# Feature exponent of a linear-attention kernel: norm, maximum and sign in one fused VectorE operation per head, with a new plan

## The chip, the core and the metric

The kernel runs on one core of one Trainium2 chip. The metric is device time in microseconds of one execution of the whole program. A core has TensorE (PE, matrix products into PSUM), VectorE (DVE), ScalarE (ACT), GpSimd (POOL) and SyncE (SP, which here issues every DMA). Each engine works through its own instructions in order, and semaphores order the engines among each other.

## The reference, cut to what matters

An attention in linear form (random exponential features) is followed by two multilayer perceptrons. Everything is float32; q and k are scaled, features are taken, and the attention output of shape 2304 x 512 passes through both perceptrons.

```python
def phi(x):                                    # x: 4 batches, 8 heads, 576 tokens, 64
    proj = np.einsum('bhsd,md->bhsm', x, omega)          # 128 features
    sq = np.sum(x * x, axis=-1, keepdims=True) / 2.0
    h = proj - sq
    h = h - np.max(h, axis=-1, keepdims=True)
    return np.exp(h) / np.sqrt(m)
q_p, k_p = (phi(q_s), phi(k_s))
kv = np.einsum('bhsm,bhsd->bhmd', k_p, v)
z = np.sum(k_p, axis=2)
num = np.einsum('bhsm,bhmd->bhsd', q_p, kv)
den = np.einsum('bhsm,bhm->bhs', q_p, z)[..., None] + 1e-06
x = num / den
h = x @ w_in;  g = h * np.tanh(log(1 + exp(h)));  x = g @ w_out      # 512 -> 2048 -> 512
h = x @ w_in2; g = h * sigmoid(h);                out = g @ w_out2
```

## The kernel before, in words

The kernel does not run in loops over the chip's time. It registers some thousands of small tasks (one or a few instructions each) with a planner, and the planner then writes them out in an order of its own.

**The attention.** There are 36 k units and 36 q units, each of 128 tokens by four heads. A k unit (`k_unit`) loads its tile (`kin`, DMA, ring of 5 buffers), sums the squares of its 4 x 64 columns per head (`sums`: on VectorE four multiplications with a running sum, L459; or on GpSimd and a VectorE reduction, L441 and L442; or on ScalarE, L451), projects it on TensorE (L500) into a PSUM bank `kpj`, and passes the bank to `softmax_part`. There VectorE takes the maximum over 128 features for each of the four heads in one reduction (L466), and two small operations on 128x4 (L469, L471) make the bias from the sum of squares and the maximum. ScalarE then takes four exponentials of 128x128 out of the PSUM bank into the SBUF buffer `kf` (L476; 4 buffers for k, 3 for q, where the buffer is `qf`). TensorE accumulates the outer products of the features with v and their sum (L511); at the end of a group `k_finish` copies the state and spreads the sums z (L532, L536, L542). A q unit (`q_unit`) is the same up to its exponential; then come the product with z and its sum, the denominator (`den`: on VectorE four multiplications with a running sum, L608; or on GpSimd, L592, with a VectorE reduction, L604), the small constant added (L616), the reciprocal (L617), the normalisation (L626 on GpSimd or VectorE, L623 on ScalarE), four transposes on TensorE (L633), and after every second unit the product with the state (L657), which gives x as a high and a low part (L667, L671).

**The perceptrons.** All float32 products are made of three passes over high and low parts (`mm3`, L275 to L277). Weights arrive as 64-bit numbers and are converted by ScalarE and VectorE (L690, L693, L698, L701) and split (L709, L711). The first perceptron's first half of hidden units (phase 0) is worked while the attention still runs, one 256-token block after another; phases 1 to 4 follow on pairs of blocks with pre-added operands (L717, L735, L849) and end at the last store.

**What sets the order.** `Plan.add` gives each task an engine, a modelled cost and a key (a due time, shifted by the table `OFF` by name or by kind). `Plan.order` walks a model of the engines: among the tasks that can start within `EPS` of the earliest one it takes that with the lowest key, no further than `HORIZON` ahead of the lowest key that is open; buffers come from rings with a fixed number of places. The model delays a VectorE task of the kinds listed in `SHARED` while GpSimd is busy, and GpSimd never. The result is a fixed order on every engine. `VAR` holds a letter for each unit that says on which engine a task of a kind is done (D VectorE, P GpSimd, A ScalarE).

Of the kernel before, what the change touches and what calls it, by code (L numbers as in the profile page):

```python
# [19 lines left out]
P = 128  # L20
# [13 lines left out]
QLEAD = 10.0  # L34
KLEAD = 20.0
KSPAN = 6.0
EPS = 0.1
NUMC = 1.2

FILL_END, FILL_MIN, FILL_PART, FILL_COST, FILL_MAX = 140.0, 0.35, 0.75, 0.12, 24  # L40
STRETCH, FALL, RISE = 3.413, 0.64, 0.93

VAR = dict(sqk="DPPDDDDDDDDAAAPPDDDDDDPPDPADDDPDDADD",
           sqq="DPDDPPDDDPDADPPDDDDPPPPDAADPDDPDDDAD",
           den="DDDDDDDDDPDDPPDPDDDDPDPPDPDPPDDDDDPP",
           fn="PPDPPPPDPPPPAPPDPPPDAPPPPPPPDAPPDAPD",
           gl="DDDDPDDPDDDPDDDDDPDPDDPDPPDDDDPPPPDD",
           qlo="PDPDPPPPDPPPDDDPDPPDPDPDPPPPPDPPPDPD",
           wl="DDPDPDDPPPPPPDDD",
           wsg="DDDDDDDDDDDDDDDDDDDDDDDDDDDDDDDDDDDDDDDDDDDDDDDDD",  # L50
           xlo="DDDDDPDDDDDPDPPDPD",
           spl="S4444S4SS4S4SSSSSSSS4SSS4SSSS4S4444S")
HORIZON = 21.0
OFF = {'H': -0.73, 'K*': -3.2, 'K0': -1.24, 'K1': -0.82, 'K10': -0.02, 'K11': 0.14, 'K12': -0.13, 'K13': -0.32, 'K14':
# [16 lines left out]
LAT = {"PE": 0.21, "ACT": 0.15, "DVE": 0.13, "Pool": 0.1, "DMA": 1.35}  # L71
ISSUE = {"DMA": 1.1}
TABLE = 1.3

SHARED = dict(wb0=1.0, wo0=1.5, ws0=1.1, wl0=0.8, wb1=1.2, wo1=2.0, ws1=1.3, gl=1.0, ksqr=2.5, qsqr=2.5, den=1.3, fn=0.8,
              qlo=0.8, xtbx=1.6, sa=2.8, kba=4.0, kbb=4.0, qba=5.0, qbb=5.0, dea=5.0)

# [15 lines left out]
class Plan:  # L93
# [8 lines left out]

    def add(self, name, eng, cost, key, fn, reads=(), writes=(), new=(), after=(), lat=None, tab=None, fill=None):
# [19 lines left out]
        self.tasks.append(dict(name=name, eng=eng, cost=cost, key=key, fn=fn, deps=deps, new=list(new), tab=tab, fill=fill, kind=kind_of(name)[0],  # L123
                               lat=LAT.get(eng, 0.0) if lat is None else lat))
        assert name not in self.index, name
        self.index[name] = i

    def order(self):
# [29 lines left out]
        while ready:  # L158
# [22 lines left out]
            first = min(min(c)[0:1] + (e,) for e, c in cand.items())  # L181
            at, i, tags = min((c for c in cand[first[1]] if c[0] <= first[0] + EPS), key=lambda c: (self.tasks[c[1]]["key"], c[0]))
            t = self.tasks[i]
# [11 lines left out]
            if t["eng"] == "PE" and at < 250:  # L195
                end = clock.run(at, t["cost"], t["fills"] * FILL_COST)
            if t["eng"] == "DVE" and t["kind"] in SHARED:
                slow = SHARED[t["kind"]]
                end += slow / (1 + slow) * max(0.0, min(t["cost"] * (1 + slow), free.get("Pool", 0.0) - at))
            if t["eng"] != "-":  # L200
# [65 lines left out]
def performer_two_mlps(ctx: ExitStack, tc: tile.TileContext, qin, kin, omT, w1, w2, out):  # L266
# [133 lines left out]

    smk = sb.tile([P, 4, 4, 4], F32, tag="smk", name="smk")
    smq = sb.tile([P, 4, 6, 4], F32, tag="smq", name="smq")
# [3 lines left out]
    def om_prep():  # L406
        om = t["cst"][:, P:P + 256]
        DVE.tensor_scalar_mul(om, om, 2.0 ** -1.5)
        DVE.tensor_copy(t["om"][:, 0:256], om)
# [23 lines left out]
    def sums(nm, src, sm, r, key, n, load):  # L433
# [6 lines left out]
        if VAR["sq" + nm][n] == "P":  # L440
# [22 lines left out]
    def softmax_part(nm, sm, r, key, n, pj, f):  # L463

        v = lambda: t[pj].rearrange("p (h m) -> p h m", m=NF)
        T(f"{nm}max{n}", "DVE", 0.6, key, lambda: DVE.tensor_reduce(sm[:, r, 1, :], v(), AX.X, ALU.max), reads=[pj],  # L466
          writes=[f"sm{nm}:{r}m"])

        T(f"{nm}ba{n}", "DVE", 0.075, key, lambda: DVE.scalar_tensor_tensor(sm[:, r, 2, :], sm[:, r, 0, :], -1.0 / 16, sm[:, r, 1, :], ALU.mult,  # L469
          ALU.add), reads=[f"sm{nm}:{r}s", f"sm{nm}:{r}m"], writes=[f"sm{nm}:{r}n"])  # L470
        T(f"{nm}bb{n}", "DVE", 0.075, key, lambda: DVE.scalar_tensor_tensor(sm[:, r, 3, :], sm[:, r, 0, :], -1.0 / 16, sm[:, r, 2, :], ALU.mult,  # L471
          ALU.subtract), reads=[f"sm{nm}:{r}s", f"sm{nm}:{r}n"], writes=[f"sm{nm}:{r}b"])

        def exps():
            for h in range(4):
                ACT.activation(t[f][:, h * NF:(h + 1) * NF], v()[:, h, :], AF.Exp, bias=sm[:, r, 3, h:h + 1])  # L476

        T(f"{nm}exp{n}", "ACT", 1.02, key, exps, reads=[pj, f"sm{nm}:{r}b"], writes=[f], new=[(f, nm + "f")], tab="E")

# [69 lines left out]
    def q_unit(n):  # L549
# [52 lines left out]
        def den():  # L602
# [3 lines left out]
            for b, a0, a1 in segs:  # L606
                for h in range(4):
                    DVE.scalar_tensor_tensor(t[fz][a0:a1, h * NF:(h + 1) * NF], t[f][a0:a1, h * NF:(h + 1) * NF], 1.0,  # L608
                                             t[f"z{b}"][a0:a1, 4 * g + h, :], ALU.mult, ALU.mult, accum_out=dn[a0:a1, h:h + 1])

# [3 lines left out]
        else:  # L614
            T(f"den{n}", "DVE", 0.6, key, den, reads=[fz], writes=[f"smq:{r}d"])
        T(f"dea{n}", "DVE", 0.08, key, lambda: DVE.tensor_scalar_add(rc, dn, 1e-6 * NF), reads=[f"smq:{r}d"], writes=[f"smq:{r}r"])  # L616
        T(f"der{n}", "DVE", 0.09, key, lambda: DVE.reciprocal(rc, rc), writes=[f"smq:{r}r"])  # L617

# [472 lines left out]
```

## Time and profile before

| | us |
|---|---|
| median of 3 runs | 951.62 |
| lowest, highest run | 951.58, 952.08 |
| span of the profiled execution (first to last instruction) | 949.4 |
| the profiled execution's own time beside its span | not recorded; the median stands 2.2 above the span |
| TensorE busy | 926.1 (98%) |
| VectorE, ScalarE, GpSimd busy | 604.0, 519.4, 325.2 |

Busy time of an engine is the time in which at least one of its instructions was running; records of successive instructions overlap a little. Idle time of an engine is put down to the instruction that released it. The granted clock of TensorE is 1.00 at its full level and 0.50 at half of it. "PEld" is the load of the stationary operand, which runs beside the products; names such as kpj, qf, smk are the program's tiles, without the buffer's number.

### The profile page before, as it was taken

Reading aid. Unit: us, or ns where it says so; the run is one execution under the profiler, and the core shown is the slowest. Engines: PE = TensorE matmul, PEld = TensorE weight load, DVE = VectorE, ACT = ScalarE, POOL = GpSimd, SP = SyncE. Lnnn points to the kernel's source line nnn. Section 1 sums busy time; section 2 is a strip of 40 time slices with the busy share of each in tenths; the row PEclk is TensorE's granted clock in tenths of the full one; section 3 lists DMA queues with packets and bytes.
Section 4 is the critical chain, followed back from the end, with each engine's and each line's share of the span. In section 5 each row is a group of like instructions: output and inputs, shape, how many; then the busy total and the mean of one; then the engine's idle time right before and its main releaser. Section 6 shows DMA issues by size and latency. Waiting matters only on the chain.

```text
span 949.4 us, 17714 instructions
## 1 busy us (share of the span) xinstructions
PE 926.1 (98%) x6513; PEld 848.2 (89%) x6513; DVE 604.0 (64%) x1606; ACT 519.4 (55%) x1167; POOL 325.2 (34%) x297
## 2 busy tenths in 40 slices
PE   7799999999999999999999999999999999999998
PEld 6678899999999999988998888989999889988998
DVE  6999868868764638574456797446556764353422
ACT  5877988787777645444234554436355454424221
POOL 1323124535542465334106374135053261303010
PEclk9899999999999999999999999999999999999999
DMA  9777342433221325340422443214222211320202
GB/s 309 240 238 242 112 146 90 118 105 123 79 81 65 101 78 162 106 142 36 134 90 67 135 133 96 90 37 159 86 67 90 67 56 52 94 89 23 89 1 89
DMA packets 50359, 102.53 MB, mean 108 GB/s; under 512 B 4961, under 2 KB 17505, under 8 KB 50273
## 3 DMA queue, kind: packets, MB, share of 16 engines
q1 hardware_dynamic: 50272, 101.41, 33.2%
q8 instruction: 51, 0.84, 0.4%
q14 instruction: 36, 0.29, 0.1%
HBM read 78.85 MB, written 22.54 MB: 107 GB/s over the span
## 4 chain that ended last, share of the span: by engine, by line
PE 81%; DVE 9%; issue 2%; DMA 2%; POOL 2%; ACT 2%; SPq 1%; DVEq 0%; POOLq 0%; ACTq 0%
PE y L275 12%; PE y L276 12%; PE y L277 12%; PE ha L275 4%; PE ha L277 4%; PE ha L276 4%; PE h L275 4%; PE h L277 4%; PE h L276 4%; PE hb L275 3%; PE hb L277 3%; PE hb L276 3%; PE acc L511 2%; PE kpj L500 2%; PE xp L657 1%
## 5 line engine op out<-in xcount | busy, mean ns | idle before, releaser
L795 ACT CAST gh<-e 128x512 fp32r<-128x512 f32 x144 | 89.3, 623 | 173.0 <-PE y L276 172.2
L797 DVE TENSOR_TENSOR gl<-e,gh 128x512 fp32r<-128x512 f32 x132 | 105.6, 807 | 122.5 <-ACT gh L795 122.4
L275 PE MATMUL y<-gh,W 128*128 128x256 f32 (+1 forms) x528 | 171.4, 325 | 0.2 <-DVE stg L931 0.2
L276 PE MATMUL y<-gh,W 128*128 128x256 f32 (+1 forms) x528 | 169.6, 321 | 0.0
L277 PE MATMUL y<-gl,W 128*128 128x256 f32 (+1 forms) x528 | 169.6, 321 | 0.0
L275 PEld LDWEIGHTS y<-gh,W 128*128 128x128 f32 x528 | 99.2, 188 | 9.2 <-issue 1.0
L277 PEld LDWEIGHTS y<-gl,W 128*128 128x128 f32 x528 | 99.1, 188 | 8.8
L276 PEld LDWEIGHTS y<-gh,W 128*128 128x128 f32 x528 | 99.2, 188 | 7.6
L275 PE MATMUL h<-X,W 128*128 128x256 f32 x288 | 83.5, 290 | 0.0
L277 PE MATMUL h<-X,W 128*128 128x256 f32 x288 | 80.4, 279 | 0.0
L276 PE MATMUL h<-X,W 128*128 128x256 f32 x288 | 80.4, 279 | 0.0
L849 DVE TENSOR_TENSOR Lfz<-Lfz,ha 128x256 f32<-128x256 f32 x48 | 20.1, 419 | 87.8 <-PE ha L277 62.9
L717 POOL TENSOR_TENSOR LHL<-Lqf,LX 128x512 fp32r<-128x512 f32 x14 | 18.3, 1311 | 141.9 <-ACT LX L716 141.3
L690 ACT ACTIVATE wa<-wr 128x512 f32<-128x512 f32 x64 | 43.4, 681 | 36.9 <-DVE wt L701 28.6
L794 ACT ACTIVATE e<-hb 128x512 f32<-128x512 f32 x48 | 28.7, 598 | 54.3 <-DVE hb L849 54.1
L275 PEld LDWEIGHTS h<-X,W 128*128 128x128 f32 x288 | 54.3, 188 | 1.0 <-ACT e L794 0.4
L276 PEld LDWEIGHTS h<-X,W 128*128 128x128 f32 x288 | 54.2, 188 | 0.2
L277 PEld LDWEIGHTS h<-X,W 128*128 128x128 f32 x288 | 54.1, 188 | 0.0
L693 DVE TENSOR_SCALAR wt<-wr 128x512 int32<-128x512 int32 x64 | 38.5, 609 | 20.7 <-POOL W L717 16.9
L701 DVE SCALAR_TENSOR_TENSOR wt<-wa,wt 128x512 int32<-128x512 int32 x64 | 50.7, 801 | 0.8
L500 PE MATMUL kpj<-cst,kin 128*128 128x256 f32 x144 | 40.9, 415 | 9.8 <-ACT qf L476 4.8
L626 POOL TENSOR_TENSOR qf<-qf,smq 128x512 f32<-128x512 f32 x25 | 27.2, 1093 | 53.1 <-DVE smq L617 17.6
(570 smaller groups left out, 2913.8 us busy)
## 6 DMA issues: line engine op xcount, KB each, us to landing
wr<-in_w_dram SPq DMA_DIRECT2D x64, 512.0 KB, 4.5
kin<-in_kin_dram SPq DMA_DIRECT2D x35, 386.0 KB, 4.4
qin<-in_qin_dram SPq DMA_DIRECT2D x36, 256.0 KB, 3.3
xf<-sx SPq DMA_DIRECT2D x18, 256.0 KB, 2.5
yp<-stg SPq DMA_DIRECT2D x18, 256.0 KB, 2.3
stg<-yp SPq DMA_DIRECT2D x18, 256.0 KB, 4.3
y<-stg SPq DMA_DIRECT2D x18, 256.0 KB, 2.4
Lqf<-y SPq DMA_DIRECT2D x17, 256.0 KB, 3.1
```

Source lines behind the costliest of these rows:

```text
L275: PE.matmul(o, s_hi, m_hi, start=first, stop=False, skip_group_check=True)
L276: PE.matmul(o, s_lo, m_hi, start=False, stop=False, skip_group_check=True)
L277: PE.matmul(o, s_hi, m_lo, start=False, stop=last, skip_group_check=True)
L500: PE.matmul(t[pj][:, jj * 256:(jj + 1) * 256], t[res][:, jj * P:(jj + 1) * P], t["cst"][:, P:P + 256], start=True, stop=True, skip_group_c ...
L626: (DVE if fn_e == "DVE" else POOL).tensor_tensor(x, x, smq[:, r, 5, :, None].to_broadcast([P, 4, NF]), ALU.mult)
L690: T("wm" + c, "ACT", 0.57, key, lambda: ACT.activation(t[wa], t[raw][:, :, 1].bitcast(F32), AF.Copy, scale=2.0 ** -112), reads=[raw], writ ...
L693: sign = dict(D=lambda: DVE.tensor_scalar(t[wt], t[raw][:, :, 1], -0x80000000, None, ALU.bitwise_and), A=lambda: ACT.activation(t[wt].bitc ...
L701: T("ws" + c, "DVE", 0.6, key, lambda: DVE.scalar_tensor_tensor(t[wt], t[wa].bitcast(I32), 3, t[wt], ALU.logical_shift_left, ALU.bitwise_o ...
L794: T(f"X{s}.{x}", "ACT", 0.49, ks, lambda: ACT.activation(t[e], t[h], AFN), reads=res, writes=[e], new=[(e, "e")], tab=tab)
L795: T(f"gh{s}.{x}", "ACT", 0.52, ks, lambda: ACT.copy(t[gh[x]], t[e]), reads=[e], writes=[gh[x]], new=[(gh[x], "ghi")])
L797: T(f"gl{s}.{x}", dict(D="DVE", P="Pool")[low], dict(D=0.605, P=1.25)[low], ks, lambda: dict(D=DVE, P=POOL)[low].tensor_tensor(t[gl[x]], t ...
L849: T(f"{nm}{s}", "DVE", 0.335, ks, lambda: DVE.tensor_tensor(q(o, ox), q(a, ax), q(b, bx), ALU.add), reads=[r for r in (res(a, ax), res(b, ...
```

## The change

It has four parts.

*The fused operation.* The prepared projection matrix is scaled by -(2^2.5) instead of 2^-1.5, sixteen times as much and with the other sign. Per head one `tensor_tensor_reduce` on VectorE reads the 128x128 projection out of PSUM, adds the head's sum of squares (broadcast along the columns), divides by 16, writes the result to the SBUF buffer of the features and takes the minimum along it. The exponential then works in place in that buffer, with scale -1 and the minimum as its bias. The reduction L466 and the two small operations L469 and L471 are gone.

```diff
-        DVE.tensor_scalar_mul(om, om, 2.0 ** -1.5)
+        DVE.tensor_scalar_mul(om, om, -(2.0 ** 2.5))
...
-        T(f"{nm}max{n}", "DVE", 0.6, key, lambda: DVE.tensor_reduce(sm[:, r, 1, :], v(), AX.X, ALU.max), reads=[pj],
-          writes=[f"sm{nm}:{r}m"])
-        T(f"{nm}ba{n}", "DVE", 0.075, ...)
-        T(f"{nm}bb{n}", "DVE", 0.075, ...)
+        v = lambda h: t[pj][:, h * NF:(h + 1) * NF]
+        o = lambda h: t[f][:, h * NF:(h + 1) * NF]
+        def shift():
+            for h in range(4):
+                DVE.tensor_tensor_reduce(out=o(h), in0=v(h), in1=sm[:, r, 0, h:h + 1].to_broadcast([P, NF]), scale=1.0 / 16, scalar=3.0e38,
+                                         op0=ALU.add, op1=ALU.min, accum_out=sm[:, r, 1, h:h + 1])
+        T(f"{nm}max{n}", "DVE", TTR, key, shift, reads=[pj, f"sm{nm}:{r}s"], writes=[f, f"sm{nm}:{r}m"], new=[(f, nm + "f")])
         def exps():
             for h in range(4):
-                ACT.activation(t[f][:, h * NF:(h + 1) * NF], v()[:, h, :], AF.Exp, bias=sm[:, r, 3, h:h + 1])
-        T(f"{nm}exp{n}", "ACT", 1.02, key, exps, reads=[pj, f"sm{nm}:{r}b"], writes=[f], new=[(f, nm + "f")], tab="E")
+                ACT.activation(o(h), o(h), AF.Exp, bias=sm[:, r, 1, h:h + 1], scale=-1.0)
+        T(f"{nm}exp{n}", "ACT", 1.1, key, exps, reads=[f"sm{nm}:{r}m"], writes=[f], tab="E")
```

*The denominator.* Where it is on VectorE, the multiplication with a running sum becomes a `tensor_tensor_reduce` whose sum starts at the small constant, so the addition L616 goes there.

```diff
-                    DVE.scalar_tensor_tensor(t[fz][a0:a1, ...], t[f][a0:a1, ...], 1.0,
-                                             t[f"z{b}"][a0:a1, 4 * g + h, :], ALU.mult, ALU.mult, accum_out=dn[a0:a1, h:h + 1])
+                    DVE.tensor_tensor_reduce(out=t[fz][a0:a1, ...], in0=t[f][a0:a1, ...],
+                                             in1=t[f"z{b}"][a0:a1, 4 * g + h, :], scale=1.0, scalar=1e-6 * NF, op0=ALU.mult, op1=ALU.add,
+                                             accum_out=dn[a0:a1, h:h + 1])
```

*The plan's model.* `SHARED` (a slowing factor by kind) is replaced by `LOCKS`: a VectorE task of a listed kind is delayed by 0.88 of what GpSimd still has to do, and a GpSimd task by 0.88 of what the VectorE instruction in hand still holds. The fused maximum is not in the list.

```diff
-            if t["eng"] == "DVE" and t["kind"] in SHARED:
-                slow = SHARED[t["kind"]]
-                end += slow / (1 + slow) * max(0.0, min(t["cost"] * (1 + slow), free.get("Pool", 0.0) - at))
+            if t["eng"] == "DVE" and t["lock"]:
+                end += LOCK * max(0.0, free.get("Pool", 0.0) - at)
+                held_to, held_for = end, t["cost"] / t["lock"]
+            if t["eng"] == "Pool":
+                end += LOCK * max(0.0, min(held_to - at, held_for))
```

*Order and engines anew.* `OFF` now holds some 500 entries, most of them for single tasks of every phase, in place of about 150 by kind; `KLEAD`, `KSPAN`, `EPS`, `HORIZON`, `XLEAD` and the due times `W1` to `W3` are shifted slightly. In `VAR`, 9 of 36 letters of `fn` change (25 to 18 units on GpSimd, 7 to 11 on VectorE, 4 to 7 on ScalarE), 13 of `gl` (12 to 21 on GpSimd, the rest on VectorE), 8 of 18 of `xlo` (5 to 9 on GpSimd), 7 of `sqq` (two units by a new letter S: the square on ScalarE in one piece, the sum on VectorE), one of `den` and one of `wl`.

```diff
-           fn="PPDPPPPDPPPPAPPDPPPDAPPPPPPPDAPPDAPD",
-           gl="DDDDPDDPDDDPDDDDDPDPDDPDPPDDDDPPPPDD",
+           fn="PADPPPPDPPPPAPDDPPDPADPPDPDADAPADAPD",
+           gl="PDDDPDDPPPDPDDDPPPDPDDPPDPPPPPDPPPDP",
...
-           xlo="DDDDDPDDDDDPDPPDPD",
+           xlo="DDPDDPPDPDDDPDPPPP",
```

## Rows read from the trace of the kernel before

**Rows 1.** The page, part 1: busy us, share of the span, instructions.
```profile
PE 926.1 (98%) x6513; PEld 848.2 (89%) x6513; DVE 604.0 (64%) x1606; ACT 519.4 (55%) x1167; POOL 325.2 (34%) x297
```

**Rows 2.** Busy time in four stretches: length, engines with counts, clock, DMA share, GB/s.
```profile
0.00:24.00 24.00, 18.72 (x106) 15.50 (x107) 16.86 (x94) 12.92 (x37) 2.79 (x10) 1.00 0.90 308
24.00:96.00 72.00, 61.73 (x412) 54.06 (x412) 71.14 (x331) 58.41 (x190) 22.99 (x24) 0.95 0.73 237
96.00:350.00 254.00, 252.07 (x2109) 239.37 (x2108) 176.72 (x612) 192.62 (x453) 105.77 (x100) 1.00 0.32 101
350.00:949.00 599.00, 593.55 (x3892) 539.28 (x3890) 339.24 (x571) 255.43 (x489) 193.68 (x164) 1.00 0.27 88
```

**Rows 3.** Waits of TensorE: line, releaser, us in total, times, longest.
```profile
PE kpj L500 <- ACT qf L476: 4.8, 2, 4.0
...
PE ha L275 <- DVE hb L849: 2.5, 4, 1.2
```

**Rows 4.** Timeline around the stall: TensorE, VectorE, ScalarE (start, length, instruction).
```profile
41.63 2.08 PE L500 MATMUL kpj<-cst,kin 128*128 128x256 f32 x4 [4.01 <-ACT qf L476]
...
38.00 0.69 DVE L466 TENSOR_REDUCE smq<-qpj 128x4 f32<-128x512 f32 x1
...
39.45 2.13 ACT L476 ACTIVATE qf<-qpj,smq 128x128 f32<-128x128 f32 x8
```

**Rows 5.** Busy time and granted clock around the stall; columns as in rows 2.
```profile
42.00:45.00 3.00, 3.00 (x12) 2.64 (x11) 2.73 (x17) 3.00 (x13) 1.65 (x4) 0.50 0.13 47
45.00:48.00 3.00, 3.00 (x15) 2.57 (x15) 3.00 (x9) 1.06 (x4) 2.52 (x3) 0.68 0.48 132
```

**Rows 6.** Timeline of VectorE without delays.
```profile
30.57 0.68 DVE L466 TENSOR_REDUCE smk<-kpj 128x4 f32<-128x512 f32 x1
31.17 0.68 DVE L701 SCALAR_TENSOR_TENSOR wt<-wa,wt 128x512 int32<-128x512 int32 x1
31.77 0.15 DVE L469 SCALAR_TENSOR_TENSOR smk<-smk 128x4 f32<-128x4 f32 x1
31.85 0.21 DVE L459 SCALAR_TENSOR_TENSOR qin<-qin 128x64 f32<-128x64 f32 x1
```

**Rows 7.** Timeline of VectorE: two pieces of a denominator.
```profile
40.67 0.28 DVE L608 SCALAR_TENSOR_TENSOR fz<-qf,z 128x128 f32<-128x128 f32 x1
...
40.88 0.28 DVE L608 SCALAR_TENSOR_TENSOR fz<-qf,z 128x128 f32<-128x128 f32 x1
```

**Rows 8.** Groups of VectorE, 24 to 96 us: count, busy us, mean ns, idle before.
```profile
L466 DVE TENSOR_REDUCE smk<-kpj 128x4 f32<-128x512 f32 x22 | 14.7, 680 | 0.3 <-PE kpj L500 0.3
...
L471 DVE SCALAR_TENSOR_TENSOR smk<-smk 128x4 f32<-128x4 f32 x22 | 4.7, 224 | 0.0
L469 DVE SCALAR_TENSOR_TENSOR smk<-smk 128x4 f32<-128x4 f32 x22 | 4.6, 217 | 0.0
L466 DVE TENSOR_REDUCE smq<-qpj 128x4 f32<-128x512 f32 x6 | 4.1, 681 | 0.0
...
L471 DVE SCALAR_TENSOR_TENSOR smq<-smq 128x4 f32<-128x4 f32 x6 | 1.8, 294 | 0.0
...
L616 DVE TENSOR_SCALAR smq<-smq 128x4 f32<-128x4 f32 x5 | 1.0, 196 | 0.0
```

**Rows 9.** Tiles smk, smq, qf, whole span: count, length in ns (least/median/longest).
```profile
L471 DVE SCALAR_TENSOR_TENSOR smk<-smk x36: 148/156/1281, 13.6 to 137.2; 128x4 f32<-128x4 f32 x36
...
L476 ACT ACTIVATE qf<-qpj,smq x144: 353/377/489, 39.5 to 307.6; 128x128 f32<-128x128 f32 x144
...
L471 DVE SCALAR_TENSOR_TENSOR smq<-smq x36: 143/162/1230, 35.5 to 306.6; 128x4 f32<-128x4 f32 x36
...
L623 ACT ACTIVATE qf<-qf,smq x16: 387/436/476, 154.8 to 302.8; 128x128 f32<-128x128 f32 x16
```

**Rows 10.** Waits from 24 to 96 us; columns as in rows 3.
```profile
POOL qf L626 <- ACT W L709: 13.0, 1, 13.0
...
ACT kf L476 <- DVE smk L471: 5.2, 5, 3.3
```

More of the change, by code (lines that the diff above doesn't have):

```diff
@@ L34 @@
 QLEAD = 10.0
-KLEAD = 20.0
-KSPAN = 6.0
-EPS = 0.1
+KLEAD = 20.025
+KSPAN = 6.021
+EPS = 0.103
 NUMC = 1.2
+TTR = 0.86
 FILL_END, FILL_MIN, FILL_PART, FILL_COST, FILL_MAX = 140.0, 0.35, 0.75, 0.12, 24
@@ L73 @@
 TABLE = 1.3
-SHARED = dict(wb0=1.0, wo0=1.5, ws0=1.1, wl0=0.8, wb1=1.2, wo1=2.0, ws1=1.3, gl=1.0, ksqr=2.5, qsqr=2.5, den=1.3, fn=0.8,
-              qlo=0.8, xtbx=1.6, sa=2.8, kba=4.0, kbb=4.0, qba=5.0, qbb=5.0, dea=5.0)
+LOCKS = dict(wb0=1, wo0=1, ws0=1, wl0=1, wb1=1, wo1=1, ws1=1, gl=1, ksqr=4, qsqr=4, den=4, fn=1, qlo=1, xtbx=1, sa=1, dea=1)
+LOCK = 0.88
 def kind_of(name):
@@ L101, in __init__, with add @@
         self.hold, self.pinned = {}, set()
-    def add(self, name, eng, cost, key, fn, reads=(), writes=(), new=(), after=(), lat=None, tab=None, fill=None):
+    def add(self, name, eng, cost, key, fn, reads=(), writes=(), new=(), after=(), lat=None, tab=None, fill=None, lock=None):
         deps = set(self.index[a] for a in after)
@@ L123, in add @@
         self.tasks.append(dict(name=name, eng=eng, cost=cost, key=key, fn=fn, deps=deps, new=list(new), tab=tab, fill=fill, kind=kind_of(name)[0],
+                               lock=lock if lock is not None else LOCKS.get(kind_of(name)[0], 0) if eng == "DVE" else 0,
                                lat=LAT.get(eng, 0.0) if lat is None else lat))
@@ L141, in order @@
         free, ready, out, table = {}, {i for i in range(n) if not need[i]}, [], "E"
-        self.loads = 0
+        self.loads, held_to, held_for = 0, 0.0, 0.0
         def slot(ring, taken):
@@ L181, in order @@
             first = min(min(c)[0:1] + (e,) for e, c in cand.items())
-            at, i, tags = min((c for c in cand[first[1]] if c[0] <= first[0] + EPS), key=lambda c: (self.tasks[c[1]]["key"], c[0]))
+            at, i, tags = min((c for c in cand[first[1]] if c[0] <= first[0] + EPS), key=lambda c: (self.tasks[c[1]]["key"], c[0], c[1]))
             t = self.tasks[i]
@@ L398, in performer_two_mlps @@
     assert not early + fresh + mid + plain + x0 + x1 + static
-    smk = sb.tile([P, 4, 4, 4], F32, tag="smk", name="smk")
+    smk = sb.tile([P, 4, 2, 4], F32, tag="smk", name="smk")
     smq = sb.tile([P, 4, 6, 4], F32, tag="smq", name="smq")
@@ L445, in sums @@
             return
+        if VAR["sq" + nm][n] == "S":
+            T(f"{nm}sqr{n}", "ACT", 0.31, key, lambda: ACT.activation(tk(), tk(), AF.Square), writes=[res + ":tk"])
+            T(f"{nm}sum{n}", "DVE", 0.335, key, lambda: DVE.tensor_reduce(
+                sm[:, r, 0, :], tk().rearrange("p (h d) -> p h d", d=HD), AX.X, ALU.add), reads=[res + ":tk"],
+              writes=[f"sm{nm}:{r}s"])
+            return
         if VAR["sq" + nm][n] == "A":
@@ L607, in den @@
                 for h in range(4):
-                    DVE.scalar_tensor_tensor(t[fz][a0:a1, h * NF:(h + 1) * NF], t[f][a0:a1, h * NF:(h + 1) * NF], 1.0,
-                                             t[f"z{b}"][a0:a1, 4 * g + h, :], ALU.mult, ALU.mult, accum_out=dn[a0:a1, h:h + 1])
+                    DVE.tensor_tensor_reduce(out=t[fz][a0:a1, h * NF:(h + 1) * NF], in0=t[f][a0:a1, h * NF:(h + 1) * NF],
+                                             in1=t[f"z{b}"][a0:a1, 4 * g + h, :], scale=1.0, scalar=1e-6 * NF, op0=ALU.mult, op1=ALU.add,
+                                             accum_out=dn[a0:a1, h:h + 1])
         if den_d:
@@ L614, in q_unit @@
         else:
-            T(f"den{n}", "DVE", 0.6, key, den, reads=[fz], writes=[f"smq:{r}d"])
-        T(f"dea{n}", "DVE", 0.08, key, lambda: DVE.tensor_scalar_add(rc, dn, 1e-6 * NF), reads=[f"smq:{r}d"], writes=[f"smq:{r}r"])
-        T(f"der{n}", "DVE", 0.09, key, lambda: DVE.reciprocal(rc, rc), writes=[f"smq:{r}r"])
+            T(f"den{n}", "DVE", 0.6, key, den, reads=[fz], writes=[f"smq:{r}d"], lock=0)
+        if den_d:
+            T(f"der{n}", "DVE", 0.09, key, lambda: DVE.reciprocal(rc, dn), reads=[f"smq:{r}d"], writes=[f"smq:{r}r"])
+        else:
+            T(f"dea{n}", "DVE", 0.08, key, lambda: DVE.tensor_scalar_add(rc, dn, 1e-6 * NF), reads=[f"smq:{r}d"], writes=[f"smq:{r}r"])
+            T(f"der{n}", "DVE", 0.09, key, lambda: DVE.reciprocal(rc, rc), writes=[f"smq:{r}r"])
         def fn():
@@ L1026, in performer_two_mlps @@
         plan.emit()
-W1, W2, W3 = (-17.7, -13.4, -3.7, 7.6), (-13.8, -1.4, 8.9, 10.1), (-3.6, -0.7, 4.7, 16.2)
-XLEAD = 5.2
+W1, W2, W3 = (-17.7, -13.4, -4.7, 5.59), (-13.8, -1.23, 6.69, 10.1), (-5.61, -3.68, 3.81, 16.87)
+XLEAD = 3.583
 _INS = ['qin', 'kin', 'omT', 'w1', 'w2']
```

21 lines of the change are left out of this document (7 added, 14 removed), and 108 rows, old and new, of the table OFF.

## The prediction

> **What bounds the kernel now.** I read the page's busy shares first: TensorE is busy 926.1 of 949.4 us [rows 1], so everything the change can win or lose in the end is TensorE idle time, 23.3 us, or slow clock. The stretches say where that lies [rows 2]. Up to 24 us TensorE idles 5.3 us while the first loads come in; the change leaves that alone. From 24 to 96 us it idles 72 - 61.73 = 10.3 us, and there VectorE is busy 71.14 of 72 us: the attention part is bound by VectorE. From 96 to 350 us TensorE idles 1.9 us while VectorE has 77 us free; after 350 us it idles 5.5 us, 2.5 of it behind one VectorE addition [rows 3].
>
> The waits of TensorE [rows 3] name the partner in the early part: ScalarE's exponentials (kpj behind qf, 4.8 us). Most of it is one stall. The projection at 41.63 us waited 4.0 us for a PSUM bank that an exponential of a q unit still had to read [rows 4]: that unit's maximum was taken at 38.00 us, its exponential ran in the pair that ScalarE began at 39.45 us. [...] So what a better early part could give is 10.3 + 2.5 = 12.8 us, and a better late part 1.9 + 2.5 = 4.4 us.
>
> **The change, part by part.**
>
> *1. The bank is freed earlier.* The fused operation writes its result to SBUF, and the exponential works there in place, so VectorE frees the bank and no longer ScalarE. In the stall [rows 4] the fused operation would end near 38.00 + 0.9 = 38.9 us and TensorE could go on at about 39.0 instead of 41.6: 2.6 us, and with a gap of 1.4 us in place of 4.0 the fall of the clock, 2.5 us, may not come. What is late next is VectorE itself, saturated around that point, so I take half: -2.5 us (bounds 0 and -5.1).
>
> *2. Maximum and two small operations become four fused ones.* On VectorE I go from start to start, since records overlap [rows 6]: the reduction of 512 columns out of PSUM occupies 31.17 - 30.57 = 0.60 us, and the next 512-wide operation, out of SBUF, also 0.60, so PSUM as a source costs nothing visible. Each small operation takes 0.08 (31.77 to 31.85). Together 0.75 us a unit, taking the second small one as 0.07. The fused operation does not occur in this trace. The nearest row is the multiplication with running sum over the same 128x128 [rows 7], with its accumulator read: 40.88 - 40.67 = 0.21 us, so 0.86 for four. Its bounds are 0.15, a quarter of the 512-column reduction [rows 6], and 0.28, the length of a record if nothing overlapped [rows 7]. I take 0.215: +0.11 us a unit. From 24 to 96 us there are 22 + 6 units [rows 8]: +3.1 us. Against it stands what the small operations lost to blocking: their means are 224 and 217 ns for k and 294 ns for one of q [rows 8], against 156 ns (median [rows 9]), 150 ns (undelayed [rows 6]) and 162 ns (median [rows 9]). That is 22 x 0.068 + 22 x 0.067 + 6 x 0.132 = 3.8 us that goes with them. If GpSimd then holds up the next two-source operation instead, nothing is saved: the part lies between -0.7 and +3.1. I take +1.0.
> [...]
>
> *3. The addition before the reciprocal goes* where the denominator is on VectorE: 5 units in the stretch [rows 8] at 0.08 us, -0.4 us.
>
> *4. ScalarE.* Exponentials now read SBUF: the nearest row is the scaling in place, median 436 ns against 377 for the exponential from PSUM [rows 9]: 4 x 0.06 = 0.24 us a unit, 28 units, 6.7 us at most and nothing at least. ScalarE has 13.6 us free in the stretch [rows 2], and its exponentials now wait for one group instead of three operations spread along VectorE's queue (kf stood 5.2 us behind the last small one [rows 10]). I set both against each other: 0, bounds +2 and -2. If ScalarE had no free time, this would cost the 6.7 us.
>
> *5. Engines and order.* Early letters nearly cancel on VectorE (one low part of x leaves it, one low part of a weight comes to it, each about 0.60 us like the 512-wide operation in rows 6). Later ones move g's low parts and some of x's to GpSimd and normalisations from GpSimd to ScalarE and VectorE, in stretches where all three have room [rows 2]. DMA issues keep their number; each still waits for the last reader of its buffer, which the change keeps. The order is decided anew for the whole kernel, with GpSimd delayed by VectorE in the plan too, which the old plan left out. Between 24 and 96 us VectorE cannot do more, but the 77 us that it has free afterwards can take work that TensorE does not need yet. How much of the 12.8 - 2.5 = 10.3 us left is won can't be read from rows; the bounds are a loss of 3 (an order that is laid on wrong lengths somewhere) and a gain of 8. I take a bit under a third, -3.0, and of the late 4.4 us -1.0.
>
> **Sum:** -2.5 + 1.0 - 0.4 + 0 - 3.0 - 1.0 = -5.9 us. The span was 949.4 us and the median time 951.62, so 2.2 us lie around the span: 949.4 - 5.9 + 2.2 = 945.7 us. The profiled execution has no time of its own beside its span, so I use this difference.
>
> **Rivals.**
> - *The gain is eaten on VectorE* (953.0). Each fused operation takes 0.28 us, as if nothing overlapped: 1.12 a unit, 0.26 more than I took, and 28 x 0.26 = 7.3 us are more than the -5.9. For it: VectorE is saturated, so every 0.01 us a piece is 1.1 us in the stretch. Against it: every 128-column row overlaps to 0.21. [...]
> - *VectorE waits for buffers* (954.7, slower). The buffer of the exponential is now taken by VectorE, not ScalarE: three for q and four for k. A fused operation whose buffer is still read (by accumulation, or by normalisation and transposition) holds up everything behind it on the saturated VectorE: squares, weights, other maxima. One normalisation on GpSimd began after 13.0 us of idle time that a cast of a weight on ScalarE ended [rows 10], so q buffers can be held long. At 1.5 us (my choice between nothing and the 4.0 us of the longest stall [rows 3]) for each of the 6 q units it is +9.0 against -5.9: +3.1. It decides from 5.9 us of new VectorE idle time before 96 us on; before, that was 0.9 [rows 2].
> - *The early stall all goes* (938.7): three quarters of 12.8 + 4.4 = 12.9 us. For it: the losses are a few long waits on one cause. Against it: VectorE's saturation stays.
> - *The bank is freed earlier but not used earlier*, because TensorE's next task waits for something else: part 1 is nil, 948.2. This lies in the range of the forecast and gets no chance of its own.
>
> **How the numbers follow.** The forecast, with 941 to 949.5 as its own range, gets 0.50; the big gain 0.17; the gain eaten 0.16; buffers 0.17. About 0.2% can be told from no change here, 949.7 to 953.5. Of the case "eaten" I count 0.01 as faster, 0.10 as the same, 0.05 as slower. Faster: 0.50 + 0.17 + 0.01 = 0.68; same 0.10; slower 0.17 + 0.05 = 0.22. The range runs from the big gain to the buffer case: 938.5 to 955.
>
> **What would show it.** Right: no wait of kpj behind an exponential, clock 1.00 from 36 to 48 us, fused operations 0.21 to 0.22 us apart, TensorE idle 5 to 8 us in 24 to 96 us, little change after 350 us. Wrong: fused operations 0.26 us apart or more; VectorE idle before a fused operation with kf's or qf's last reader as the releaser; an early part that wins but a late part that loses as much, which would mean that the new order and not the fused operation set the time.

## The result, and the profile after

The changed kernel takes 943.55 us (median of 4, 941.05 to 946.98) against 951.85 us before, a ratio of 0.9916 with a 95% interval of 0.9894 to 0.9938. A second set of executions gave 943.44 us (6 executions, 941.65 to 947.48) against 951.58, ratio 0.9919 [0.9904, 0.9935]. So it is 8 us faster, and its executions scatter over 6 us where those of before stay within 1 to 3.

The page of the kernel after, part 1 (columns as in [rows 1]):

```profile
PE 936.0 (99%) x6531; PEld 861.9 (91%) x6531; DVE 592.9 (63%) x1914; ACT 530.9 (56%) x1179; POOL 335.2 (35%) x303
```

Its busy time by stretch (columns as in [rows 2]):

```profile
0.00:24.00 24.00, 20.82 (x101) 18.40 (x102) 16.27 (x125) 12.96 (x34) 2.65 (x9) 0.86 0.88 303
24.00:96.00 72.00, 70.03 (x437) 62.57 (x437) 66.23 (x446) 62.58 (x194) 19.94 (x21) 0.88 0.68 217
96.00:350.00 254.00, 253.18 (x2115) 241.45 (x2114) 177.05 (x777) 199.00 (x465) 117.81 (x109) 1.00 0.33 106
350.00:945.20 595.20, 591.96 (x3884) 539.47 (x3883) 333.38 (x570) 256.40 (x489) 194.81 (x165) 1.00 0.27 89
```

Against [rows 2], TensorE's idle time in the second stretch fell from 10.3 to 72 - 70.03 = 2.0 us, and VectorE is no longer saturated there: 5.8 us idle instead of 0.9. Over the whole span TensorE idles 9.2 us in place of 23.3. But the column of the clock got worse: 0.86 and 0.88 in the first two stretches, which loses 24 x 0.14 + 72 x 0.12 = 12.0 us against full clock; before it was 72 x 0.05 = 3.6. Together, idle time and slow clock fell from 26.9 to 21.2 us, 5.7 less. The difference of the two spans is smaller, 949.4 - 945.2 = 4.2 us, in part because some of the idle time was not filled with work. The plan puts idle products, whose result nobody reads, in front of gaps that it foresees; they count as busy. All 18 products that came with the change are such (line, operation, tiles, shape, count; busy us, mean ns, idle before). Before:

```profile
L422 PE MATMUL xp<-om 128*128 128x256 f32 x5 | 0.8, 298 | 0.0
L422 PE MATMUL acc<-om 128*128 128x248 f32 x4 | 0.7, 303 | 0.0
```

After:

```profile
L508 PE MATMUL acc<-om 128*128 128x248 f32 x20 | 3.2, 299 | 0.0
L508 PE MATMUL tp<-om 128*128 128x256 f32 x7 | 1.7, 374 | 0.0
```

That is 4.9 us in place of 1.5, so some 3 of the 14.1 us by which idle time fell are idle products. These sums close only to about 2 us.

After 350 us TensorE idles 595.20 - 591.96 = 3.2 us, where it idled 5.9 to the end of the span before. This is more than half of the 4.2 us by which the profiled executions differ.

The profiled execution is the slowest of its four (946.98 us, mean clock 0.987); the fastest, 941.05 us, had 0.998. So the trace shows about half of the 8 us by which the medians differ. Between these two executions the mean clock alone would make 945 x 0.011 = 10.4 us, and the time differs by 5.9: part of what a slow clock costs was waiting time anyway (an estimate from these four numbers).

TensorE's waits between 24 and 350 us after (columns as in [rows 3]); in this execution none is for an exponential any more:

```profile
PE kpj L594 <- DVE qin L552: 1.0, 1, 1.0
PE acc L605 <- DVE smk L563: 0.8, 1, 0.8
PE qpj L362 <- DVE HL L663: 0.7, 1, 0.7
```

The wait of ha behind hb, 2.5 us in [rows 3], is gone too.

The fused operation in the timeline of VectorE after, two pieces of one unit:

```profile
32.49 0.28 DVE L563 CUSTOM_DVE_ANT_0 kf<-kpj,smk 128x128 f32<-128x128 f32 x1
32.70 0.08 DVE L563 DVE_READ_ACCUMULATOR2_ANT smk<- 128x1 f32 x1
32.70 0.28 DVE L563 CUSTOM_DVE_ANT_0 kf<-kpj,smk 128x128 f32<-128x128 f32 x1
```

And by tile, the pieces of k and of q and the exponentials of q (count; length in ns, least/median/longest; first and last start):

```profile
L563 DVE CUSTOM_DVE_ANT_0 kf<-kpj,smk x144: 270/284/293, 10.7 to 134.5; 128x128 f32<-128x128 f32 x144
...
L563 DVE CUSTOM_DVE_ANT_0 qf<-qpj,smq x144: 271/286/295, 36.7 to 300.0; 128x128 f32<-128x128 f32 x144
L570 ACT ACTIVATE qf<-qf,smq x144: 384/388/415, 45.4 to 300.9; 128x128 f32<-128x128 f32 x144
```

A piece takes 32.70 - 32.49 = 0.21 us, with its accumulator read, as the nearest row of before had it [rows 7]. And none of 288 pieces took over 295 ns, whereas the small operations that it replaces went up to 1281 [rows 9]. GpSimd was as busy as before (335.2 us against 325.2): a small operation that is left in the changed kernel, the addition behind the 13 denominators on GpSimd, still goes up to 1264 ns.

```profile
L714 DVE TENSOR_SCALAR smq<-smq x13: 165/522/1264, 127.1 to 303.7; 128x4 f32<-128x4 f32 x13
```

In the trace of before, each of the 25 of those 144 small operations that took over 1.6 times the least ran beside a GpSimd instruction. In the trace of after, 80 of the 288 pieces did and none was stretched.

In this execution the clock falls three times, in the stretches that start at 0, 36 and 72 us. The granted clock in 2 us pieces around the second fall (columns as in rows 2):

```profile
40.00:42.00 2.00, 1.39 (x13) 1.25 (x12) 2.00 (x20) 2.00 (x8) 0.00 (x0) 1.00 0.96 363
42.00:44.00 2.00, 1.57 (x10) 1.22 (x10) 1.78 (x15) 2.00 (x7) 0.00 (x0) 1.00 1.01 281
44.00:46.00 2.00, 2.00 (x16) 1.79 (x15) 0.32 (x1) 1.66 (x6) 0.61 (x1) 0.62 0.91 331
46.00:48.00 2.00, 2.00 (x8) 1.62 (x7) 2.00 (x15) 0.63 (x3) 0.88 (x1) 0.50 0.94 299
```

TensorE idled 1.0 us before its projection at 42.43 us, by the profile behind a square on VectorE (the first wait above); the clock then shows the lower level, 0.50, although TensorE is busy all the time. A stall a quarter as long as that of before [rows 4] was followed by the same fall [rows 5].

### The profile page after: what moved, and what is told of

The parts are those of the page before. It is cut to its first block, busy times and chain, and to the rows that moved or that the text cites. A ratio compares the mean times of both kernels' runs of the same rounds, so it can differ in the third digit from the quotient of the medians.

```text
span 945.2 us, 18039 instructions
## 1 busy us (share of the span) xinstructions
PE 936.0 (99%) x6531; PEld 861.9 (91%) x6531; DVE 592.9 (63%) x1914; ACT 530.9 (56%) x1179; POOL 335.2 (35%) x303
## 4 chain that ended last, share of the span: by engine, by line
PE 91%; DVE 3%; DMA 3%; ACT 1%; issue 1%; SPq 0%; POOL 0%; POOLq 0%; DVEq 0%
PE y L361 14%; PE y L363 14%; PE y L362 14%; PE ha L361 5%; PE ha L362 5%; PE ha L363 5%; PE h L361 4%; PE h L363 4%; PE h L362 4%; PE hb L361 4%; PE hb L363 4%; PE hb L362 4%; PE acc L605 3%; PE kpj L594 3%; PE xp L755 2%; PE tp L731 2%
## 5 line engine op out<-in xcount | busy, mean ns | idle before, releaser
L895 DVE TENSOR_TENSOR gl<-e,gh 128x512 fp32r<-128x512 f32 x123 | 98.5, 809 | 127.0 <-ACT gh L893 125.0
L563 DVE CUSTOM_DVE_ANT_0 qf<-qpj,smq 128x128 f32<-128x128 f32 x144 | 32.9, 286 | 28.0 <-PE qpj L363 17.6
L605 PEld LDWEIGHTS acc<-kin,kf 128*128 128x128 f32 (+1 forms) x320 | 43.2, 210 | 3.4 <-ACT FT L737 1.2
L570 ACT ACTIVATE qf<-qf,smq 128x128 f32<-128x128 f32 x144 | 45.0, 391 | 0.7 <-DVE smq L563 0.6
```

The source lines that it names most:

```text
L563: DVE.tensor_tensor_reduce(out=o(h), in0=v(h), in1=sm[:, r, 0, h:h + 1].to_broadcast([P, NF]), scale=1.0 / 16, scalar=3.0e38, op0=ALU.add, ...
L570: ACT.activation(o(h), o(h), AF.Exp, bias=sm[:, r, 1, h:h + 1], scale=-1.0)
L605: PE.matmul(a[:, h, :], t[f][r0:r1, h * NF:(h + 1) * NF], v[r0:r1, h, :], start=first and h == 0, stop=last, skip_group_check=True)
L895: T(f"gl{s}.{x}", dict(D="DVE", P="Pool")[low], dict(D=0.605, P=1.25)[low], ks, lambda: dict(D=DVE, P=POOL)[low].tensor_tensor(t[gl[x]], t ...
```

## The experiments

My theory after the result: the time came from the order, and the fused operation only made that order possible. The rivals: the operation gains by itself (no blocking by GpSimd, bank freed earlier), or the better model of the plan does.

**Fused operation, order of before held, result in PSUM.**

```diff
+    x = t[pj][:, h * NF:(h + 1) * NF]
+    DVE.tensor_tensor_reduce(out=x, in0=x, in1=..., accum_out=sm[:, r, 1, h:h + 1])     # at the place of the first small operation
-    DVE.tensor_reduce(...); DVE.scalar_tensor_tensor(...); DVE.scalar_tensor_tensor(...)
```

> The kernel before with the fused operation in place of the maximum and the two small operations, written back into the PSUM bank, so that the exponential reads PSUM as before; TensorE, ScalarE, GpSimd and the DMA queue keep the order of the kernel before exactly. If the order is what gains (my theory), the operation alone is worth between -1 and +2 us: 951 to 954 us. If the fused operation itself gains, because the small operations no longer stand behind GpSimd, it is clearly under 949 us. VectorE's four pieces should be 0.21 us apart, as in the changed kernel.

Measured: 980.24 us, ratio 1.0303 [1.0290, 1.0317]. Both were wrong, for a reason that neither named. VectorE's timeline of that run:

```profile
31.10 0.30 DVE L470 CUSTOM_DVE_ANT_0 kpj<-kpj,smk 128x128 f32<-128x128 f32 x1
31.32 0.14 DVE L470 DVE_READ_ACCUMULATOR2_ANT smk<- 128x1 f32 x1
31.50 0.30 DVE L470 CUSTOM_DVE_ANT_0 kpj<-kpj,smk 128x128 f32<-128x128 f32 x1
...
31.89 0.30 DVE L470 CUSTOM_DVE_ANT_0 kpj<-kpj,smk 128x128 f32<-128x128 f32 x1
32.10 0.14 DVE L470 DVE_READ_ACCUMULATOR2_ANT smk<- 128x1 f32 x1
32.10 0.33 DVE L470 CUSTOM_DVE_ANT_0 kpj<-kpj,smk 128x128 f32<-128x128 f32 x1
```

Inside a unit, where a piece works in the same PSUM bank as the one before it, the pieces are 31.50 - 31.10 = 0.40 us apart (0.39 in others), and the accumulator read takes 0.14 instead of 0.08. Behind the fourth piece (31.89) the next instruction starts after 0.21 us as usual, here the first piece of another unit. That is 3 x 0.39 + 0.21 = 1.38 us a unit where 0.86 was meant, 28 x 0.52 = 15 us in the bound stretch; the kernel lost 29 us in all, and the exponentials held the bank as before, now later (over the whole span those of k waited 15.4 us behind the pieces, against 7.5 us behind the small operations before). So this run says nothing on the operation as the change uses it. It does suggest the price: what VectorE is given there comes out in the time.

**Fused operation, order of before held, result in SBUF.** A scratch of three buffers takes the result, so that nothing else moves. The four pieces stand where the first small operation stood, by the trace of before 1.3 us (k) and 1.2 us (q) after the maximum's start in the median, so the bank is freed later than a fused operation in the maximum's place would free it.

```diff
-    x = t[pj][...]; DVE.tensor_tensor_reduce(out=x, in0=x, ...)
+    s = scr[f] = sb.tile([P, DM], F32, tag=f"scr{len(scr) % 3}", name=...)
+    DVE.tensor_tensor_reduce(out=s[:, ...], in0=t[pj][:, ...], ...)          # the exponential reads s and writes t[f]
```

> The kernel before with the fused operation writing to a scratch of three buffers in SBUF, from which the exponential reads, so that the PSUM bank is free after VectorE; TensorE, ScalarE, GpSimd and the DMA queue keep the order of the kernel before exactly. The pieces should be 0.21 us apart again instead of the 0.39 that they took with PSUM as their destination. If the fused operation and the earlier bank are worth nothing without a new order (my theory): 950 to 956 us. If they gain by themselves and the order of the run with the old tables was what lost: 948 us or less.

Measured: 957.52 us, ratio 1.0070 [1.0056, 1.0083]. The pieces are 0.21 us apart again and never delayed. Yet by themselves, at this place, the operation and the earlier bank lose 6.5 us, slightly more than my range. The stretch from 24 to 96 us of this kernel:

```profile
24.00:96.00 72.00, 62.78 (x344) 55.51 (x343) 63.88 (x416) 53.84 (x171) 20.58 (x21) 0.79 0.66 217
```

Its pieces of k, by tile:

```profile
L470 DVE CUSTOM_DVE_ANT_0 scr<-kpj,smk x144: 260/285/292, 10.6 to 146.3; 128x128 f32<-128x128 f32 x144
```

And the waits of TensorE in it between 24 and 96 us:

```profile
PE acc L515 <- ACT kf L480: 2.3, 1, 2.3
PE kpj L504 <- DVE smq L470: 2.2, 1, 2.2
PE xp L661 <- ACT FT L643: 2.0, 1, 2.0
PE kpj L504 <- ACT z L546: 1.2, 1, 1.2
PE zt L540 <- ACT zb L536: 1.1, 1, 1.1
```

VectorE now has 8.1 us free there, and TensorE idles 9.2 us, 1.1 less than before, and stands at a clock of 0.79. The bank no longer waits for an exponential, and other waits stand in its place: these five are 8.8 of the 9.2 us, four of them (6.6 us) behind ScalarE. The profiled execution is the slowest of six (960.59 us, mean clock 0.984): its slow clock loses 72 x 0.21 = 15.1 us where 3.6 were lost before, more than its extra time (spans of 958.8 and 949.4 us). But the execution with a mean clock of 0.995, as high as that of the kernel before, took 956.04 us, still 5 us more than the kernel before beside it (950.99); where these 5 us lie stays open, as only the slowest execution has a trace. That an order that suited the old operations does not use what the new one frees fits both, and is not shown apart from the late place of the pieces.

**Fused operation with the tables of before, order worked out anew.** The old model and due times, the fused operation and its result in SBUF as in the change.

```diff
 HORIZON = 21.0                # OFF, VAR, SHARED, lead times: as before
+TTR = 0.86                    # softmax_part and the matrix's factor: as in the change
```

> The kernel before with the fused operation and its result in SBUF, so that the PSUM bank is free after VectorE; due times, engine letters and the plan's model of before, order worked out anew from them. If the earlier release gains by itself, 945 to 947 us and no wait of a projection behind an exponential. If it gains only with the new due times (my theory), 948 to 952 us: that wait goes, but another one of the same size takes its place.

Measured: 968.62 us, ratio 1.0187 [1.0174, 1.0200]: worse than either expected. The waits that lost are late ones:

```profile
PE tp L635 <- POOL qf L628: 7.0, 5, 2.3
PE h L276 <- ACT e L796: 4.4, 3, 2.3
...
PE ha L276 <- DVE hb L851: 2.5, 4, 1.2
```

The wait of a projection behind an exponential is gone, as both expected. From 96 to 350 us TensorE idles 254 - 240.19 = 13.8 us, where it idled 1.9 before.

**The changed kernel with the tables of before.** It adds the two-way blocking and the fused denominator to the last one.

```diff
-KLEAD = 20.025; KSPAN = 6.021; EPS = 0.103; OFF = {... some 500 ...}; VAR = dict(... new letters ...)
+KLEAD = 20.0;   KSPAN = 6.0;   EPS = 0.1;   OFF = {... as before ...}; VAR = dict(... as before ...)
```

> The changed kernel with the due times, lead times and engine letters of before; so against the last one it has the two-way blocking in the plan's model and the denominator's fused form. If the better model gains by itself, 945 us or less. If the tables do (my theory), within 2 us of the last kernel, and 4 us or more above the changed one.

Measured: 959.12 us, ratio 1.0084 [1.0071, 1.0097]. The new model does not gain by itself against the kernel before, and the tables are worth 15.6 us more. I had expected it within 2 us of the last kernel; it is 9.5 better. One part of that is the model's. The stretch after 350 us, of the last kernel and then of this one:

```profile
350.00:966.70 616.70, 610.69 (x4041) 556.48 (x4039) 347.85 (x579) 262.52 (x504) 205.49 (x175) 1.00 0.27 87
350.00:957.30 607.30, 604.19 (x3992) 551.84 (x3990) 342.28 (x579) 261.08 (x499) 201.19 (x173) 1.00 0.28 88
```

TensorE idles 6.0 us there in the last kernel and 3.1 in this one, and the wait of ha behind hb, 2.5 us, is gone. The same split runs through all kernels of this document: the five with the old model, whatever their operations and order, idle 5.9 to 6.0 us after 350 us and have that wait (2.3 to 2.5 us); the eight traces with the new model, old tables and the undone denominator included, idle 3.1 to 3.5 us and have 0.3 us of it or none. So 2 to 3 of the 8 us that the change gains go with the plan's new model alone (which also breaks ties in its own way). Whether the other 6 to 7 us between these two kernels are the model's, or one unfitted order is simply luckier than another, stays open: the controls below move the time as far.

**The changed kernel with the three operations of before.**

```diff
-    T(f"{nm}max{n}", "DVE", TTR, key, shift, ...)
+    T(f"{nm}max{n}", "DVE", 0.6, ...); T(f"{nm}ba{n}", ...); T(f"{nm}bb{n}", ...)     # model, VAR and OFF: new; due times of ba and bb: as before
```

> The changed kernel with the maximum and the two small operations of before in place of the fused one, and so the bank held until the exponential has read it; due times, letters and the plan's model are the new ones. If the order alone gains, 943 to 946 us. If the new order rests on the fused operation (my theory), half the gain or more is gone: 947 us or more, with waits behind exponentials between 24 and 96 us.

Measured: 971.56 us, ratio 1.0212 [1.0187, 1.0238]. The waits behind exponentials are there between 24 and 96 us (3.7 us of TensorE). The new tables without the operation lose more than the operation without the tables. The old operations in the new order itself were not tried: that order hands a bank on before the exponential that would read it.

**Two controls.** One lead time of the plan is shifted by 0.1, in the kernel before and in the one after.

```diff
-KLEAD = 20.0          # before                -KLEAD = 20.025        # after
+KLEAD = 20.1                                  +KLEAD = 20.125
```

> A control: the kernel before with one lead time of the plan, that of the k units, at 20.1 instead of 20.0; nothing else. If any order that was not fitted loses as much as the runs with half of the change did: 958 us or more. If orders near the fitted one are as good: 950 to 954 us, and the losses of those runs came from what they changed.

> The same control on the changed kernel: the k lead time at 20.125 instead of 20.025. If the gain of the change rests on an order fitted to each task: 950 us or more, so that the gain is gone. If it rests on the operation and the engines' letters: 942 to 947 us.

Measured: 960.16 us for the first, ratio 1.0093 [1.0073, 1.0114], and 954.91 us for the second, 1.0044 [1.0031, 1.0056]. With every operation, cost and letter as it was (the second has six idle products fewer), an order a little beside the fitted one loses 9 us before and 11 us after: as much as the whole change gains. Two stretches of the second kernel:

```profile
24.00:96.00 72.00, 65.84 (x423) 58.10 (x423) 66.64 (x466) 63.53 (x196) 20.20 (x21) 0.93 0.71 231
96.00:150.00 54.00, 47.66 (x352) 43.28 (x351) 50.21 (x289) 44.89 (x128) 17.78 (x17) 0.95 0.44 136
```

And waits of its TensorE over the whole span, which show what an unfitted order loses to:

```profile
PE kpj L594 <- DMA kin<-in_kin_dram: 4.0, 3, 3.0
PE h L361 <- ACT e L892: 4.0, 1, 4.0
PE acc L605 <- ACT kf L570: 2.4, 2, 2.1
```

So the losses of the runs with half of the change can't be read as prices of what each left out. The runs that hold the order come nearer to a price, but only within an order that was fitted to something else. One rival is left untested: that a longer fit of the old operations, with some 500 due times in place of 150, would have gained as much.

**Idle products in front of three stalls**, to see what the clock costs.

```diff
+WARMER = {"kproj19": ("kacc12.0", 7), "kacc22.1": ("kacc21.0", 6)}     # products whose result nobody reads
-            if t["fills"]:
-                t["fill"](t["fills"])
+            if t["fills"] or t["name"] == "kproj3":
+                t["fill"](t["fills"] or 14)
```

> The changed kernel with idle products of TensorE in front of three of its stalls (14 before the fourth projection of k, 7 and 6 before the two stalls near 42 and 69 us), every other instruction as it was. If the falls of the clock behind these stalls cost what the trace says, the mean clock rises to 0.997 or more and the time falls to 938 to 941 us, with less scatter. If VectorE sets the pace behind the stalls anyway, the clock rises and the time stays at 942 to 944 us.

Measured: 941.76 us (941.10 to 942.53), ratio 0.9901 [0.9889, 0.9914], mean clocks of 0.996 to 0.998. The median lies between the two ranges expected; the scatter fell to 1.4 us.

**The changed kernel again, beside the next two.**

> The changed kernel as it is, on the same chip as the next two kernels, so that they can be compared with it: 942 to 945 us, with a mean clock between 0.987 and 0.998 and the longer times at the lower clocks.

Measured: 943.44 us, as told above. Its slowest execution, 947.48 us, had 0.989; 941.65, 942.74 and 943.42 us had 0.996.

**The denominator undone, order held.**

```diff
-    DVE.tensor_tensor_reduce(out=t[fz][...], ..., scalar=1e-6 * NF, op0=ALU.mult, op1=ALU.add, accum_out=...)
+    DVE.scalar_tensor_tensor(t[fz][...], ..., 1.0, ..., ALU.mult, ALU.mult, accum_out=...)
-    DVE.reciprocal(rc, dn)
+    DVE.tensor_scalar_add(rc, dn, 1e-6 * NF); DVE.reciprocal(rc, rc)
```

> The changed kernel with the denominator's product and sum, the added constant and the reciprocal of before; the order on TensorE, ScalarE, GpSimd and the DMA queue is that of the changed kernel. If this part is worth what I gave it (0.08 us a unit on VectorE, 0.4 us in the bound stretch), the time stays within 2 us of the changed kernel's. If a short operation between two fused ones stalls behind GpSimd and holds up the chain, 946 us or more.

Measured: 945.53 us, ratio 0.9936 [0.9925, 0.9948], against 0.9919 [0.9904, 0.9935] for the changed kernel beside it. The medians lie 2.1 us apart, between the two cases expected, and the intervals overlap. At the same mean clock of 0.996 its three executions (944.67, 945.53, 945.84) all lie above those three of the changed kernel, by 2.7 us in the mean. By tile, the addition that came back:

```profile
L711 DVE TENSOR_SCALAR smq<-smq x23: 140/163/1264, 46.7 to 299.5; 128x4 f32<-128x4 f32 x23
```

It has the long delays that the other small operations had in [rows 9], but only 3 of the 23 are long (1.9 us together, from the trace), and each ran beside a GpSimd instruction. Which wait of TensorE they lengthen is not shown.

**Idle products in front of five stalls.**

```diff
-WARMER = {"kproj19": ("kacc12.0", 7), "kacc22.1": ("kacc21.0", 6)}
+WARMER = {"kproj19": ("kacc12.0", 7), "kproj17": ("kacc15.1", 7), "kacc22.1": ("kacc21.0", 6)}
+MORE = {"kproj3": 14, "tr3": 14}
```

> The changed kernel with idle products of TensorE in front of five stalls: the three of the last run with them, 7 more before the stall near 48 us and 14 more before the transposes near 72 us, where that run still showed the lower clock. If the clock is what is left to win, it stays at 0.998 or more and the time is 939 to 941.5 us in every execution. If the products now delay work that TensorE could have done, 942 us or more.

Measured: 942.00 us (940.87 to 942.20), ratio 0.9897 [0.9882, 0.9911], mean clocks of 0.999 to 1.000. Its stretches from 36 to 84 us, and those of the changed kernel below:

```profile
36.00:48.00 12.00, 11.73 (x81) 10.35 (x80) 11.02 (x80) 11.59 (x43) 3.80 (x6) 1.00 0.90 289
48.00:60.00 12.00, 11.50 (x86) 9.98 (x85) 12.00 (x104) 10.91 (x35) 1.91 (x4) 1.00 0.46 133
60.00:72.00 12.00, 12.00 (x89) 11.31 (x89) 10.55 (x68) 8.83 (x24) 2.60 (x4) 1.00 0.70 229
72.00:84.00 12.00, 11.68 (x82) 9.99 (x81) 12.00 (x68) 11.25 (x36) 5.59 (x5) 1.00 0.73 226
```

```profile
36.00:48.00 12.00, 10.96 (x68) 9.62 (x67) 10.10 (x69) 10.29 (x40) 3.52 (x4) 0.85 0.92 307
48.00:60.00 12.00, 12.00 (x72) 11.04 (x71) 11.19 (x111) 10.71 (x34) 2.30 (x3) 0.86 0.37 114
60.00:72.00 12.00, 11.14 (x82) 9.56 (x81) 10.89 (x65) 10.33 (x29) 2.49 (x3) 0.99 0.86 260
72.00:84.00 12.00, 11.94 (x52) 9.54 (x52) 10.18 (x56) 8.03 (x22) 4.35 (x4) 0.58 0.62 214
```

The clock stays full, and the time is that of the changed kernel's better executions, no lower: with no slow clock left, VectorE and ScalarE are up to 12.00 and 11.59 of 12 us busy, so they may set the pace. The other case expected is not excluded: the time is at its bound of 942 us, and the 48 further idle products occupy TensorE for some 6 to 7 us (an estimate: 14 in a row take 2.02 us in the trace of the run with three stalls), in which work may have had to wait. Both kernels with idle products have lower medians than the changed one, and no execution above 942.6 us, but their intervals overlap with its own.

## Why the prediction was right, and where not

The sign, the size (945.7 forecast, 943.55 measured) and the range held. The mechanism was right in outline: most of the idle time was in the early VectorE-bound stretch, the stall on the bank went, and so did the blocking. But that the size came so near is luck: the terms were off by more than the whole gain and cancelled. Step by step:

- *Part 1, the bank* (-2.5): the wait went, but as a gain of its own the step failed. With the order of before held and the bank freed early, parts 1, 2 and 4, which I had summed to -1.5 us, came to +6.5 us: TensorE found five other waits and the clock fell further. I treated the parts as terms that add; in the old order they did not, with the pieces in the place of the first small operation. The fourth rival, a bank that is freed earlier and not used earlier (948.2), is nearest to that kernel in kind, but it put the part at nil and not at a loss.
- *Part 2, the fused operation* (+1.0): the size of a piece was exact, 0.21 us, and the blocking did vanish. What was wrong is the sign: with the order held VectorE is busy 599.8 us over the whole span instead of 604.0 [rows 1], so over all 72 units the part gave 4.2 us of VectorE back, where I had it cost 1.0 in the stretch. A single record is 284 ns long by the median and overlaps the next: from start to start a piece out of PSUM takes 0.21 us.
- *Part 3, the denominator* (-0.4): too small. Undone with the order held it costs 2.1 to 2.7 us. I had priced only VectorE's time in the bound stretch, but all 23 units carry the addition, and it can take 1.26 us beside GpSimd; that a chain waits for it then is likely, not shown.
- *Part 4, ScalarE* (0, at most +6.7): a record of an exponential is 388 ns by the median from SBUF against 377 from PSUM [rows 9], but records overlap on ScalarE too. From start to start it is 0.292 us against 0.249 (medians in the traces), and four in a row take 1.26 us where they took 1.13 (before, then after):

```profile
79.93 1.13 ACT L476 ACTIVATE kf<-kpj,smk 128x128 f32<-128x128 f32 x4
90.22 1.26 ACT L570 ACTIVATE kf<-kf,smk 128x128 f32<-128x128 f32 x4
```

  So the part costs ScalarE 4 x 0.043 x 28 = 4.8 us in the stretch, the upper part of the 0 to 6.7. ScalarE had the room for it; four of the five waits with the order held are behind ScalarE.
- *Part 5, the order* (-4.0): this is the term that was mis-sized most. From the kernel that holds the old order (957.52) to the changed one (943.5) are 14 us, of which the denominator is 2 to 3; the rest, 11 to 12 us, came with the plan's model, order and letters, and a shift of one lead time by 0.1 takes 11 of it away. Of the late 4.4 us I forecast 1.0 and "little change after 350 us"; the late idle time fell by 3.7 us (7.8 to 4.1, to the ends of the spans), 2.6 of it after 350 us, and that goes with the model. The two errors, parts 1 and 5, cancelled.
- *The clock*: I forecast 1.00 from 36 to 48 us; it shows 0.85 there and 0.58 from 72 to 84 us in the profiled execution. I had taken a gap of 1.4 us as perhaps too short for a fall; it fell after 1.0 us. TensorE idles 2.0 us between 24 and 96 us, less than the 5 to 8 I named; part of that was given back as slow clock, and part is idle products. The 2.5 us of slow clock in the 12.8 us and in part 1 are 3 x 0.5 + 3 x 0.32, from the clocks of 0.50 and 0.68 around the stall [rows 5]; the changed kernel lost 12.0 us that way up to 96 us in its slowest execution.
- *The rivals*: "eaten on VectorE" fell with 0.21 us a piece; the run with pieces of 0.39 us lost 29 us, though it also held the bank. "Buffers" did not decide: from 24 to 96 us VectorE idles 5.8 us, 4.9 more than before and under the 5.9 from which that rival counted, and in the whole trace fused operations waited 2.4 us for a transposition and 0.9 us for an exponential. The 13.0 us on which I leaned there [rows 10] are idle time of GpSimd before a normalisation, and do not say how long a buffer was held. "The early stall all goes" (938.7) is 5 us below the result: the early idle time did go, but slow clock and idle products took its place.

What stays open: which of the new letters and due times carry the gain, since each change of one makes another order; how much of the 9.5 us between the two kernels with old tables is the model, beyond the 3 us after 350 us; and whether the old operations with an order fitted as long would have gained too. That the early gain comes from a fitted order which needs the fused operation is therefore in part argued: neither half gained alone, but neither half alone was fitted.

## What to carry to other kernels

Where a planner has been fitted to its tables, a change of an operation can't be judged by planning anew with the old tables: both orders that were shifted a little lost here about what the change gains (9 and 11 us against 8), so hold the order, or fit again, and run a control with a meaningless shift. Then compare stretch by stretch across all kernels: a part that comes back the same in every order, as the late 3 us did, can be priced although the totals can't. A fused operation that reads only one [128, 1] operand from SBUF replaced short ones that took up to 1281 ns beside a busy GpSimd, and none of its pieces took over 295; give it an SBUF destination (in place in PSUM its pieces stood 0.39 us apart, not 0.21), then the bank is free as well, and count what the reader behind it pays for that (here 0.292 us an exponential in place of 0.249). Take the price of an operation from start to start: the records overlap and hide it (a piece is 284 ns long and the next starts after 0.21 us). Once stalls are short, look at the clock of every execution: a few idle products in front of the last stalls kept the clock up (means of 0.996 to 1.000) and all executions at 942.6 us or less.

## What was not expected of the hardware

- Pieces of 128x128 with an accumulator start 0.21 us apart from PSUM to SBUF. In place in PSUM they start 0.39 to 0.40 us apart inside a unit, that is in the same bank, with the accumulator read at 0.14 in place of 0.08 us, and 0.21 to 0.22 before an instruction that works elsewhere. A destination in another bank than the source was not tried.
- The exponential from SBUF starts every 0.292 us, from PSUM every 0.249, while the records differ by 11 ns only.
- None of the 288 pieces out of PSUM was delayed (at most 295 ns), though 80 of them ran beside GpSimd instructions, which stretched operations on 128x4 in SBUF to 1264 ns in the same trace.
- The same program ran at mean clocks from 0.987 to 0.998, which goes with 941 to 947.5 us; the lower clock followed a stall of 1.0 us.
